# Attention and a two-expert router on one core: the two heads of a pair in one product of 128 rows, with block-diagonal keys and values

## The chip, the cores and the metric

The kernel runs on one core of one Trainium2 chip. A core has five engines that work side by side and signal one another with semaphores: TensorE (PE, matrix products, with weight loads shown as PEld), VectorE (DVE), ScalarE (ACT), GpSimd (POOL) and SyncE (SP), and 16 DMA engines that move data between the chip's memory, the on-chip memory SBUF and the product memory PSUM. The metric is the time of one execution in microseconds. Before the change it is 391.89 us, the median of 3 runs (388.24 to 396.87 us).

## The reference: what is computed

Two stages. The first is attention over 4 batches of 8 heads, 768 positions and 64 features. Positions are cut into 24 chunks of 32 queries. A chunk sees 8 memory keys of its batch and head and a window of 56 positions (16 to its left, its own 32, 8 to its right), cut off at the ends of the sequence:

```python
k_full = np.concatenate([mem_k, k_ctx], axis=2)
v_full = np.concatenate([mem_v, v_ctx], axis=2)
scores = scale * np.matmul(q_c, k_full.transpose(0, 1, 3, 2))
scores = scores - np.max(scores, axis=-1, keepdims=True)
a = np.exp(scores)
a = a / (np.sum(a, axis=-1, keepdims=True) + 1e-09)
out[:, :, c_start:c_end] = np.matmul(a, v_full)
```

The second stage takes the result as 3072 tokens of 512 features. Each token gets 8 noisy logits from two small matrices and given noise, and keeps the best two experts. The output is the sum of those two experts' results, `relu(x @ w1[e]) @ w2[e]` with 1024 hidden features, weighted by the softmax over the two logits.

## The kernel before

**Tiles.** A tile of attention is 256 positions of one batch (two groups of 128, index j) with all 8 heads, so there are 3 tiles a batch and 12 in all. Index i counts tiles, b = i // 3 is the batch and tp = i % 3 the tile in it. Heads go in 4 pairs; in SBUF the first head of a pair (par 0) has its 64 features on partitions 0 to 63, the second (par 1) on partitions 64 to 127.

**Loading.** Values, keys and queries of a batch are loaded in their natural layout by `load_batch` (lines 111 to 114). Keys and queries are turned by `turn` (lines 368 to 378), one unit for each pair, 4 units of keys and 4 of queries: 12 transposes of 128 positions by 64 features into PSUM, then a copy into `kT` or `qT`. Values take a way of their own: `spread_v` (line 347) copies them on POOL into `vp` with the heads in another order, `window_v` (line 353) stores them to a buffer `vd` in the chip's memory and loads them again, so that each chunk's window of 56 positions and its 8 memory values stand on partitions: the first heads of the pairs on partitions 0 to 63 of `vb`, the second heads on 64 to 127.

**A tile's work.** `scores` (line 380) has, for each j and pair, two products with the memory keys (one for each head) and eight with the keys: 4 chunks by 2 heads, each 64 rows (features) by 32 queries by 56 keys, placed at their own rows and columns of the array. A tile has 80 products. DVE then takes the maximum of each row and subtracts it, ACT takes the exponential (`exps`), PE turns the probabilities (`turn_p`), and `values` (line 426) multiplies them with `vb`: 64 products of 64 rows by 32 queries by 64 features, then a division by the sums (line 447) that writes `xrow`. `keep_x` (line 473) stores the rows of a tile to the chip's memory as `xd` for the experts, `turn_x` and `gate` compute the logits, and `Route` computes, batch by batch, which tokens go to which pair of experts.

**Order.** The order on PE, ACT, DVE and SP is the order of the program, written out by hand (line 504). The loop of lines 515 to 555 interleaves: in iteration i it computes the scores of tile i + 1, turns the probabilities of tile i, does the rest of tile i - 1, and the values of tile i. The query units of batch b + 1 are turned in iteration tp = 2, ahead of the scores of tile i + 1 (lines 525 to 528); its key units in tp = 1, behind the values (lines 543 to 546). POOL's DMA issues are kept in the order of the program too. There are two buffers each of `kT`, `qT`, `vb`, of the natural keys and queries `nat`, and of `xrow`, used in turn by even and odd batches. A framework that knows which instruction writes and reads which part of memory adds the waits, in the order of the program.

**Weights and scratch.** The weights of all 8 experts have one large tile, `w_all`: 65,536 columns of two bytes on 128 partitions, 8192 a expert, the first half of them for w1 and the second for w2. Attention's buffers `xrow`, `vb`, `vp`, `vn` and `nat` are cut from the upper end of the same tile (`scratch`, lines 94 to 103), from column 65536 downwards in the order in which they are named. Three experts are loaded while attention still runs, in iterations 6, 7 and 8 by the program's order:

```python
            if i in range(2 * TP, 2 * TP + 3):
                load_expert(i - 2 * TP)
            if tp == TP - 1 and b + 1 < B:
                for u in range(HP, 2 * HP):
                    o_, i_ = turn(b + 1, u)
```

The others are loaded from the end of the routing on. Then the experts' stage gathers tokens from `xd` (line 607), turns them (line 627) and runs two products for each expert (lines 646 and 655).

Of the kernel before, what the change touches and what calls it, by code (L numbers as in the profile page):

```python
# [22 lines left out]
def kernel(  # L23
# [14 lines left out]
    nc = tc.nc  # L38
    B, H, S, D = q.shape
# [30 lines left out]
    def pin(i):  # L70
        tc.keep_in_program_order(i)
# [32 lines left out]
    first_late = scol[0] // WE  # L104

    vd = [tc.dram_tile([S + CH, Dm], BF16, name=f"vd{i}") for i in range(2)]

# [22 lines left out]
    zeros = keep.tile([LC, Dm], BF16, name="zeros")  # L130
    nc.vector.memset(zeros, 0.0)
    for i in range(2):
        for r0, n in ((0, LC), (LC + S, CH - LC)):
# [7 lines left out]
    mvs = keep.tile([B * NM, H, D], F32, name="mvs")  # L141
# [55 lines left out]
    for i in range(2):  # L197
        nc.vector.memset(kT[i][:, :, 0:LC], 0.0)
        nc.vector.memset(kT[i][:, :, LC + S:SP], 0.0)

    mkT = keep.tile([128, HP, B * NM], BF16, name="mkT")
# [6 lines left out]
    nc.vector.tensor_copy(mkT, p_mk.rearrange("p c x b m -> p c (x b m)"))  # L208

    class Route:  # L210
        def __init__(self, g0, n, lg):
# [141 lines left out]
    def window_v(b):  # L353
        t, o = vb[b % 2], vd[b % 2]
        nc.sync.dma_start(out=o[LC:LC + S, :].rearrange("(p s) c -> p (s c)", s=SO), in_=vp)
        for par in range(2):
            p0 = par * 64
            cols = slice(par * 256, (par + 1) * 256)
            pin(nc.gpsimd.dma_start(out=t[p0:p0 + NM], in_=mvn[b * NM:(b + 1) * NM, cols].unsqueeze(1).to_broadcast([NM, NCH, 256])))
        for par in range(2):  # L360
            p0 = par * 64
            cols = slice(par * 256, (par + 1) * 256)
            for r0, n in ((0, CH), (CH, WIN - CH)):
                pin(nc.gpsimd.dma_start(out=t[p0 + NM + r0:p0 + NM + r0 + n],  # L364
                                        in_=o[r0:r0 + S, cols].rearrange("(c k) w -> k c w", k=CH)[0:n]))


    def turn(b, unit):
        x, pair = divmod(unit, HP)
        src = nat[b % 2][x]  # L370
        p_t = psT.tile([128, SO, 128], BF16, name="p_t", tag="ps_t")
        for s in range(SO):
            for par in range(2):
                nc.tensor.transpose(out=p_t[par * 64:par * 64 + 64, s, :],  # L374
                                    in_=src[:, 2 * pair + par, s * D:(s + 1) * D],
                                    identity=identb, tile_position=(0, par * 64))
        dst = qT[b % 2][:, pair, :] if x else kT[b % 2][:, pair, LC:LC + S]
        return dst.rearrange("c (p s) -> c p s", s=SO), p_t.rearrange("c s p -> c p s")

    def scores(t):  # L380
        b, tp = divmod(t, TP)
        q_, k_ = qT[b % 2], kT[b % 2]
        ps_s = psS.tile([128, 2, 2, HP, KW], F32, name="ps_s")
        for j in range(2):
            for pair in range(HP):
                tk = (2 * tp + j) * 128
                for par in range(2):
                    rows = slice(par * 64, par * 64 + 64)
                    nc.tensor.matmul(out=ps_s[:, par, j, pair, 0:NM], lhsT=q_[rows, pair, tk:tk + 128],  # L389
                                     rhs=mkT[rows, pair, b * NM:(b + 1) * NM], start=True, stop=True,  # L390
                                     tile_position=(par * 64, 0))
                for r in range(4):
                    for par in range(2):
                        rows = slice(par * 64, par * 64 + 64)
                        tr = tk + r * CH
                        nc.tensor.matmul(out=ps_s[r * CH:(r + 1) * CH, par, j, pair, NM:KW],  # L396
                                         lhsT=q_[rows, pair, tr:tr + CH],
                                         rhs=k_[rows, pair, tr:tr + WIN], start=True, stop=True,
                                         tile_position=(par * 64, r * CH))
        if tp == 0:  # L400
            nc.vector.memset(ps_s[0:CH, :, 0, :, NM:NM + LC], NEG)
        if tp == TP - 1:
            nc.vector.memset(ps_s[128 - CH:128, :, 1, :, KW - RC:KW], NEG)
        s3 = ps_s.rearrange("p a j c w -> p (a j c) w")
        mx = work.tile([128, 2 * H], F32, name="mx")
        nc.vector.tensor_reduce(out=mx, in_=s3, axis=AX, op=Alu.max)  # L406
        sc = work.tile([128, 2 * H, KW], F32, name="sc")
        nc.vector.tensor_tensor(out=sc, in0=s3, in1=bc(mx, KW), op=Alu.subtract)  # L408
        return sc

    def exps(sc):
        pb = work.tile([128, 2 * HP, 2, KW], BF16, name="pb")
        nc.scalar.activation(out=pb.rearrange("p x a w -> p a x w"), in_=sc.rearrange("p (a x) w -> p a x w", a=2),
                             func=Act.Exp, scale=scale)
        return pb

    def turn_p(pb):
# [8 lines left out]
    def values(t, pT, between=None):  # L426
        b, tp = divmod(t, TP)
        ps_g = psG.tile([128, 2, H], F32, name="ps_g", tag="ps_g")
        for x in range(2 * HP):
            j, pair = divmod(x, HP)  # L430
            nc.tensor.matmul(out=ps_g[:, j, 2 * pair:2 * pair + 2], lhsT=pT[:, x, :], rhs=ones2,
                             start=True, stop=True)
        ps_o = psO.tile([128, 2, 2, HP, D], F32, name="ps_o")
# [10 lines left out]
        nc.vector.reciprocal(rs, ps_g)  # L444
        xr = xrow[b % 2][:, 2 * tp:2 * tp + 2]
        for j in range(2):
            nc.vector.tensor_tensor(out=xr[:, j, 0:Dm].rearrange("p (c a d) -> p a c d", c=HP, a=2), in0=ps_o[:, :, j],  # L447
                                    in1=bc(rs[:, j].rearrange("p (c a) -> p a c", a=2), D), op=Alu.mult)
            if j == 0 and between is not None:
                between()  # L450
        return xr
# [52 lines left out]
    with tc.manual_schedule(engines={ET.PE, ET.Activation, ET.DVE, ET.SP}):  # L504
        spread_v(0)
        window_v(0)
        for u in range(2 * HP):
            o_, i_ = turn(0, u)
            (nc.scalar.copy if u % 2 else nc.vector.tensor_copy)(o_, i_)
        load_batch(1)  # L510
        spread_v(1)
        pbs[0] = exps(scores(0))
# [2 lines left out]
        for i in range(NT):  # L515
# [8 lines left out]
                load_expert(i - 2 * TP)  # L524
            if tp == TP - 1 and b + 1 < B:
                for u in range(HP, 2 * HP):
                    o_, i_ = turn(b + 1, u)
                    (nc.scalar.copy if u % 2 else nc.vector.tensor_copy)(o_, i_)
            if i + 1 < NT:
                sc = scores(i + 1)  # L530
# [11 lines left out]
            xrs[i] = values(i, pTs.pop(i), last)  # L542
            if tp == 1 and b + 1 < B:
                for u in range(HP):
                    o_, i_ = turn(b + 1, u)
# [352 lines left out]
```

## Time and profile before

| what | value |
|---|---|
| median of 3 runs | 391.89 us (388.24 to 396.87) |
| the profiled execution | 393.52 us |
| its span | 391.8 us, 8846 instructions |
| PE busy | 307.5 us (78%), 3868 products |
| DVE busy | 169.3 us (43%) |
| ACT busy | 120.2 us (31%) |
| POOL busy | 129.5 us (33%) |
| moved by DMA | 54.07 MB, mean 138 GB/s |
| score products with keys, line 396 | 768, busy 24.3 us |
| score products with memory keys, line 389 | 192, busy 17.9 us |
| value products, line 439 | 768, busy 10.0 us |
| key copies after the first batch, line 546 | 12, busy 8.7 us |

Engines overlap, so their busy times don't add up to the span, and a busy time is an average over stages. What counts is which wait ends last in each stage. A group is named by its line, engine and operation, with out<-in by the program's names. In a timeline or a chain, idle time is put down to its releaser, the event that ended it; "issue" is idle time in which the engine waited for nothing that the profile shows. A granted clock of 1.0 is TensorE's full speed.

### The profile page before, as it was taken

Reading aid. Unit: us, or ns where it says so; the run is one execution under the profiler, and the core shown is the slowest. Engines: PE = TensorE matmul, PEld = TensorE weight load, DVE = VectorE, ACT = ScalarE, POOL = GpSimd, SP = SyncE. Lnnn points to the kernel's source line nnn. Section 1 sums busy time; section 2 is a strip of 40 time slices with the busy share of each in tenths; the row PEclk is TensorE's granted clock in tenths of the full one; section 3 lists DMA queues with packets and bytes.
Section 4 is the critical chain, followed back from the end, with each engine's and each line's share of the span. In section 5 each row is a group of like instructions: output and inputs, shape, how many; then the busy total and the mean of one; then the engine's idle time right before and its main releaser. Section 6 shows DMA issues by size and latency. Waiting matters only on the chain.

```text
span 391.8 us, 8846 instructions
## 1 busy us (share of the span) xinstructions
PE 307.5 (78%) x3868; PEld 199.1 (51%) x3868; DVE 169.3 (43%) x393; ACT 120.2 (31%) x182; POOL 129.5 (33%) x168
## 2 busy tenths in 40 slices
PE   0267765866758455379999999999988999999991
PEld 0256654755646343246555446666445666555540
DVE  2345444867657369734123411595321134313230
ACT  1122633540452323013432143312224411244310
POOL 6353234325520003476236522063272023201122
PEclk9999965565585555559999999999999999999997
DMA  9999999999999992039999970712039941100012
GB/s 125 238 141 189 213 157 222 219 150 217 204 182 218 217 205 66 12 98 190 240 209 247 228 153 14 122 44 95 24 114 173 210 97 73 68 5 2 21 43 74
DMA packets 42957, 54.07 MB, mean 138 GB/s; under 512 B 7607, under 2 KB 33271, under 8 KB 42912
## 3 DMA queue, kind: packets, MB, share of 16 engines
q0 software_dynamic: 34240, 46.82, 66.1%
q10 hardware_dynamic: 7136, 3.02, 3.6%
q1 hardware_dynamic: 1536, 3.61, 2.5%
q8 instruction: 32, 0.52, 0.5%
q14 instruction: 13, 0.11, 0.1%
HBM read 70.39 MB, written 13.96 MB: 215 GB/s over the span
## 4 chain that ended last, share of the span: by engine, by line
PE 30%; issue 17%; DMA 5%; POOL 4%; DVE 3%; POOLq 1%
PE p_h L646 16%; PE p_y L655 12%; DMA out_dram<-y,main_dst 5%; POOL out_dram L613 2%; PE p_xt L627 1%; POOL xt L607 1%; DMA xt<-xd,main_src 1%; POOL w_all L771 0%; POOL w_all L770 0%; DVE w_all L447 0%; POOLq L893 0%; DVE oh_l L306 0%; DVE c L227 0%; DVE mm L224 0%; DVE c L229 0%
## 5 line engine op out<-in xcount | busy, mean ns | idle before, releaser
L655 PE MATMUL p_y<-w_all,h 128*128 128x512 bf16 x464 | 103.9, 379 | 2.4 <-ACT y L659 2.4
L646 PE MATMUL p_h<-xTt,w_all 128*128 128x384 bf16 (+2 forms) x640 | 102.3, 319 | 0.0
L646 PEld LDWEIGHTS <-w_all 128*128 128x128 bf16 x704 | 66.8, 99 | 38.0 <-issue 2.1
L634 ACT ACTIVATE h<-p_h 128x512 bf16<-128x512 f32 (+1 forms) x82 | 44.7, 545 | 102.9 <-PE p_h L646 90.7
L655 PEld LDWEIGHTS <-h 128*128 128x128 bf16 x464 | 44.9, 98 | 53.5 <-issue 2.7
L632 DVE TENSOR_SCALAR h<-p_h 128x512 bf16<-128x512 f32 (+1 forms) x50 | 31.3, 626 | 89.4 <-PE p_h L646 86.4
L613 POOL DMA_INDIRECT out_dram<-y,main_dst x28 | 31.1, 1110 | 104.1 <-DVE y L661 84.0
L661 DVE SCALAR_TENSOR_TENSOR y<-p_y,main_w,y 128x512 f32<-128x512 f32 x28 | 21.0, 750 | 37.4 <-PE p_y L655 32.3
L607 POOL DMA_INDIRECT xt<-xd,main_src x28 | 27.3, 975 | 25.4 <-PE p_xt L627 16.1
L396 PE MATMUL ps_s<-kT,qT 64*32 64x56 bf16 x768 | 24.3, 220 | 13.3 <-issue 13.3
L374 PE MATMUL p_t<-identb,w_all 128*64 128x128 bf16 x384 | 20.8, 295 | 15.4 <-DMA w_all<-in_k_dram 8.2
L659 ACT ACTIVATE y<-p_y,main_w 128x512 f32<-128x512 f32 x28 | 19.1, 687 | 41.0 <-PE p_y L655 35.1
L423 ACT COPY pT<-p_p 128x1024 bf16<-128x1024 bf16 x12 | 12.1, 1012 | 58.2 <-PE p_p L420 58.2
L374 PEld LDWEIGHTS <-w_all 128*64 128x64 bf16 x384 | 18.7, 160 | 16.5 <-DMA w_all<-in_k_dram 8.3
L349 POOL COPY w_all<-w_all 128x1536 bf16<-128x1536 bf16 x8 | 13.0, 1658 | 35.0 <-DMA w_all<-in_v_dram 35.0
L389 PE MATMUL ps_s<-mkT,qT 64*128 64x8 bf16 x192 | 17.9, 184 | 4.4 <-DVE sc L408 2.9
L364 POOL DMA_DIRECT2D w_all<-vd x16 | 11.9, 748 | 25.0 <-DMA vd<-w_all 25.0
L406 DVE TENSOR_REDUCE mx<-ps_s 128x16 f32<-128x1024 f32 x12 | 14.7, 1223 | 8.9 <-PE ps_s L396 8.6
L447 DVE TENSOR_TENSOR w_all<-ps_o,rs 128x512 bf16<-128x512 f32 x24 | 15.6, 686 | 6.6 <-PE ps_o L439 6.0
L439 PE MATMUL ps_o<-w_all,pT 64*32 64x64 bf16 x768 | 10.0, 233 | 9.8 <-issue 9.8
L396 PEld LDWEIGHTS <-qT 64*32 64x32 bf16 x768 | 11.8, 96 | 11.2 <-issue 9.6
L389 PEld LDWEIGHTS <-qT 64*128 64x128 bf16 x192 | 10.0, 100 | 14.2 <-issue 5.8
(163 smaller groups left out, 300.3 us busy)
## 6 DMA issues: line engine op xcount, KB each, us to landing
w_all<-in_moe_w_dram POOLq DMA_DIRECT2D x16, 1024.0 KB
w_all<-in_moe_w_dram POOLq DMA_DIRECT2D x8, 512.0 KB
w_all<-in_v_dram POOLq DMA_DIRECT2D x4, 768.0 KB
w_all<-in_k_dram POOLq DMA_DIRECT2D x4, 768.0 KB
w_all<-in_q_dram POOLq DMA_DIRECT2D x4, 768.0 KB
vd<-w_all SPq DMA_DIRECT2D x4, 768.0 KB, 7.4
w_all<-vd POOLq DMA_DIRECT2D x8, 384.0 KB
xd<-w_all ACTq DMA_DIRECT2D x11, 256.0 KB, 7.6
```

The source lines that it names most:

```text
L374: nc.tensor.transpose(out=p_t[par * 64:par * 64 + 64, s, :], in_=src[:, 2 * pair + par, s * D:(s + 1) * D], identity=identb, tile_position ...
L389: nc.tensor.matmul(out=ps_s[:, par, j, pair, 0:NM], lhsT=q_[rows, pair, tk:tk + 128], rhs=mkT[rows, pair, b * NM:(b + 1) * NM], start=True ...
L396: nc.tensor.matmul(out=ps_s[r * CH:(r + 1) * CH, par, j, pair, NM:KW], lhsT=q_[rows, pair, tr:tr + CH], rhs=k_[rows, pair, tr:tr + WIN], s ...
L447: nc.vector.tensor_tensor(out=xr[:, j, 0:Dm].rearrange("p (c a d) -> p a c d", c=HP, a=2), in0=ps_o[:, :, j], in1=bc(rs[:, j].rearrange("p ...
L607: i = nc.gpsimd.indirect_dma_start(out=xts[key].bitcast(I32), out_offset=None, in_=xd, in_offset=bass.IndirectOffsetOnAxis(ap=ix, axis=0))
L613: i = nc.gpsimd.indirect_dma_start(out=out, out_offset=bass.IndirectOffsetOnAxis(ap=ix, axis=0), in_=y, in_offset=None, bounds_check=N - 1 ...
L632: nc.vector.tensor_scalar(out=out_, in0=in_, scalar1=0.0, scalar2=None, op0=Alu.max)
L634: nc.scalar.activation(out=out_, in_=in_, func=Act.Relu)
L646: nc.tensor.matmul(out=o, lhsT=w(kp * F + f * 128, 128), rhs=x[:, kp], start=(kp == 0), stop=(kp == KP - 1))
L655: nc.tensor.matmul(out=p, lhsT=h[:, (f * n + j) * 128:(f * n + j + 1) * 128], rhs=w(KP * F + f * Dm, Dm), start=(f == 0), stop=(f == FB - 1))
L659: nc.scalar.activation(out=y, in_=p, func=Act.Copy, scale=weight)
L661: nc.vector.scalar_tensor_tensor(out=y, in0=p, scalar=weight, in1=y, op0=Alu.mult, op1=Alu.add)
```

## The change

Both heads of a pair go into one product whose 128 rows are the features (for values: the keys) of both heads. For this the keys `kT`, the memory keys `mkT` and the values `vb` get a further index for the head and are block-diagonal: the part of head 0 is zero on partitions 64 to 127, the part of head 1 on partitions 0 to 63. A product's output then has both heads side by side: 16 columns for memory keys, 112 for keys, 128 for values. The zeros are written once at the start. `kT` and `qT` become one buffer each, `vb` doubles, `vp` and the small staging tile `mvs` change places between the scratch and memory of their own, and a turned unit of keys is copied in two halves. The layouts of the scores and of the values' result follow.

```diff
     xrow = [scratch(SO * Dm).rearrange("p (s r) -> p s r", s=SO) for _ in range(2)]
-    vb = [scratch(NCH * HP * D).rearrange("p (c w) -> p c w", c=NCH) for _ in range(2)][::-1]
-    vp = scratch(H * SO * D)
     vn = scratch(H * SO * D).rearrange("p (h c) -> p h c", h=H)
+    vb = [scratch(2 * NCH * HP * D).rearrange("p (a c w) -> p a c w", a=2, c=NCH) for _ in range(2)][::-1]
     nat = [[scratch(H * SO * D).rearrange("p (h c) -> p h c", h=H) for _ in range(2)] for _ in range(2)]
...
+    vp = keep.tile([128, H * SO * D], BF16, name="vp")
...
-    kT = [keep.tile([128, HP, SP], BF16, name=f"kT{i}") for i in range(2)]
-    qT = [keep.tile([128, HP, S], BF16, name=f"qT{i}") for i in range(2)]
...
+    kT = keep.tile([128, HP, 2, SP], BF16, name="kT")
+    qT = keep.tile([128, HP, S], BF16, name="qT")
+    for par in range(2):
+        nc.vector.memset(kT[own(par), :, 1 - par, :], 0.0)
+        nc.vector.memset(kT[own(par), :, par, 0:LC], 0.0)
+        nc.vector.memset(kT[own(par), :, par, LC + S:SP], 0.0)
+        nc.vector.memset(vb[0][own(par), 1 - par], 0.0)
+        nc.scalar.copy(vb[1][own(par), 1 - par].rearrange("p (x c) w -> p x (c w)", x=NCH // 2),
+                       zeros[own(par), :].unsqueeze(1).to_broadcast([64, NCH // 2, Dm]))
...
-        dst = qT[b % 2][:, pair, :] if x else kT[b % 2][:, pair, LC:LC + S]
-        return dst.rearrange("c (p s) -> c p s", s=SO), p_t.rearrange("c s p -> c p s")
+        i = p_t.rearrange("c s p -> c p s")
+        if x:
+            return [(qT[:, pair, :].rearrange("c (p s) -> c p s", s=SO), i)]
+        return [(kT[own(par), pair, par, LC:LC + S].rearrange("c (p s) -> c p s", s=SO), i[own(par)]) for par in range(2)]
...
-                for par in range(2):
-                    rows = slice(par * 64, par * 64 + 64)
-                    nc.tensor.matmul(out=ps_s[:, par, j, pair, 0:NM], lhsT=q_[rows, pair, tk:tk + 128],
-                                     rhs=mkT[rows, pair, b * NM:(b + 1) * NM], start=True, stop=True,
-                                     tile_position=(par * 64, 0))
+                nc.tensor.matmul(out=ps_s[:, j, pair, :, 0:NM], lhsT=qT[:, pair, tk:tk + 128],
+                                 rhs=mkT[:, pair, :, b * NM:(b + 1) * NM], start=True, stop=True)
                 for r in range(4):
-                    for par in range(2):
-                        rows = slice(par * 64, par * 64 + 64)
-                        tr = tk + r * CH
-                        nc.tensor.matmul(out=ps_s[r * CH:(r + 1) * CH, par, j, pair, NM:KW],
-                                         lhsT=q_[rows, pair, tr:tr + CH],
-                                         rhs=k_[rows, pair, tr:tr + WIN], start=True, stop=True,
-                                         tile_position=(par * 64, r * CH))
+                    tr = tk + r * CH
+                    nc.tensor.matmul(out=ps_s[r * CH:(r + 1) * CH, j, pair, :, NM:KW], lhsT=qT[:, pair, tr:tr + CH],
+                                     rhs=kT[:, pair, :, tr:tr + WIN], start=True, stop=True, tile_position=(0, r * CH))
...
                 for r in range(4):
-                    for par in range(2):
-                        rows = slice(par * 64, par * 64 + 64)
-                        nc.tensor.matmul(out=ps_o[r * CH:(r + 1) * CH, par, j, pair, :],
-                                         lhsT=pT[rows, j * HP + pair, r * CH:(r + 1) * CH],
-                                         rhs=vb[b % 2][rows, (tp * 2 + j) * 4 + r, pair * D:(pair + 1) * D],
-                                         start=True, stop=True, tile_position=(par * 64, r * CH))
+                    nc.tensor.matmul(out=ps_o[r * CH:(r + 1) * CH, j, pair], lhsT=pT[:, j * HP + pair, r * CH:(r + 1) * CH],
+                                     rhs=vb[b % 2][:, :, (tp * 2 + j) * 4 + r, pair * D:(pair + 1) * D],
+                                     start=True, stop=True, tile_position=(0, r * CH))
...
             if tp == 1 and b + 1 < B:
                 for u in range(HP):
-                    o_, i_ = turn(b + 1, u)
-                    nc.scalar.copy(o_, i_)
+                    for o_, i_ in turn(b + 1, u):
+                        nc.scalar.copy(o_, i_)
```

More of the change, by code (lines that the diff above doesn't have):

```diff
@@ L129 @@
     make_identity(nc, identb)
-    zeros = keep.tile([LC, Dm], BF16, name="zeros")
+    vp = keep.tile([128, H * SO * D], BF16, name="vp")
+    zeros = keep.tile([128, Dm], BF16, name="zeros")
     nc.vector.memset(zeros, 0.0)
@@ L193, in bc, with own @@
         return ap.unsqueeze(len(ap.shape)).to_broadcast(list(ap.shape) + [n])
-    kT = [keep.tile([128, HP, SP], BF16, name=f"kT{i}") for i in range(2)]
-    qT = [keep.tile([128, HP, S], BF16, name=f"qT{i}") for i in range(2)]
[L197 to L201, printed above, removed]
+    def own(par):
+        return slice(par * 64, par * 64 + 64)
+    kT = keep.tile([128, HP, 2, SP], BF16, name="kT")
[7 more added lines that the diff above has]
+                       zeros[own(par), :].unsqueeze(1).to_broadcast([64, NCH // 2, Dm]))
+    mkT = keep.tile([128, HP, 2, B * NM], BF16, name="mkT")
+    nc.vector.memset(mkT, 0.0)
     p_mk = psT.tile([128, HP, 2, 2, NM], F32, name="p_mk", tag="ps_t")
@@ L207 @@
                              start=True, stop=True, tile_position=(0, par * 64))
-    nc.vector.tensor_copy(mkT, p_mk.rearrange("p c x b m -> p c (x b m)"))
+    for par in range(2):
+        nc.vector.tensor_copy(mkT[own(par), :, par, :], p_mk[own(par)].rearrange("p c x b m -> p c (x b m)"))
     class Route:
@@ L358, in window_v @@
             cols = slice(par * 256, (par + 1) * 256)
-            pin(nc.gpsimd.dma_start(out=t[p0:p0 + NM], in_=mvn[b * NM:(b + 1) * NM, cols].unsqueeze(1).to_broadcast([NM, NCH, 256])))
+            pin(nc.gpsimd.dma_start(out=t[p0:p0 + NM, par], in_=mvn[b * NM:(b + 1) * NM, cols].unsqueeze(1).to_broadcast([NM, NCH, 256])))
         for par in range(2):
@@ L363, in window_v @@
             for r0, n in ((0, CH), (CH, WIN - CH)):
-                pin(nc.gpsimd.dma_start(out=t[p0 + NM + r0:p0 + NM + r0 + n],
+                pin(nc.gpsimd.dma_start(out=t[p0 + NM + r0:p0 + NM + r0 + n, par],
                                         in_=o[r0:r0 + S, cols].rearrange("(c k) w -> k c w", k=CH)[0:n]))
@@ L373, in turn @@
             for par in range(2):
-                nc.tensor.transpose(out=p_t[par * 64:par * 64 + 64, s, :],
-                                    in_=src[:, 2 * pair + par, s * D:(s + 1) * D],
+                nc.tensor.transpose(out=p_t[own(par), s, :], in_=src[:, 2 * pair + par, s * D:(s + 1) * D],
                                     identity=identb, tile_position=(0, par * 64))
-        dst = qT[b % 2][:, pair, :] if x else kT[b % 2][:, pair, LC:LC + S]
-        return dst.rearrange("c (p s) -> c p s", s=SO), p_t.rearrange("c s p -> c p s")
+        i = p_t.rearrange("c s p -> c p s")
+        if x:
+            return [(qT[:, pair, :].rearrange("c (p s) -> c p s", s=SO), i)]
+        return [(kT[own(par), pair, par, LC:LC + S].rearrange("c (p s) -> c p s", s=SO), i[own(par)]) for par in range(2)]
     def scores(t):
         b, tp = divmod(t, TP)
-        q_, k_ = qT[b % 2], kT[b % 2]
-        ps_s = psS.tile([128, 2, 2, HP, KW], F32, name="ps_s")
+        ps_s = psS.tile([128, 2, HP, 2, KW], F32, name="ps_s")
         for j in range(2):
@@ L412, in exps @@
         pb = work.tile([128, 2 * HP, 2, KW], BF16, name="pb")
[L413 to L414 removed]
+        nc.scalar.activation(out=pb.rearrange("p x a w -> p (x a) w"), in_=sc, func=Act.Exp, scale=scale)
         return pb
@@ L432, in values @@
                              start=True, stop=True)
-        ps_o = psO.tile([128, 2, 2, HP, D], F32, name="ps_o")
+        ps_o = psO.tile([128, 2, HP, 2, D], F32, name="ps_o")
         for j in range(2):
@@ L507 @@
         for u in range(2 * HP):
-            o_, i_ = turn(0, u)
-            (nc.scalar.copy if u % 2 else nc.vector.tensor_copy)(o_, i_)
+            for n, (o_, i_) in enumerate(turn(0, u)):
+                (nc.scalar.copy if (u + n) % 2 else nc.vector.tensor_copy)(o_, i_)
         load_batch(1)
@@ L526 @@
                 for u in range(HP, 2 * HP):
-                    o_, i_ = turn(b + 1, u)
+                    o_, i_ = turn(b + 1, u)[0]
                     (nc.scalar.copy if u % 2 else nc.vector.tensor_copy)(o_, i_)
```

13 lines of the change are left out of this document (6 added, 7 removed).

## The prediction, made before the changed kernel had run

> **What bounds the kernel now.** I read the page's slices first, to divide the span into stages; then the chain that ended last, to see which wait ends each; then the timelines of PE and POOL around the last batch, and the stretches in which the DMA runs dry. The profiled execution took 393.52 us (span 391.8 us); the median of the three runs is 391.89 us, within their spread of 388.24 to 396.87. I work in the span's time and add the difference to the median.
>
> ```profile
> PE   0267765866758455379999999999988999999991
> PEclk9999965565585555559999999999999999999997
> DMA  9999999999999992039999970712039941100012
> ```
>
> A slice is 9.8 us. Attention fills slices 0 to 15: DMA full, PE broken up. From slice 18 the experts run PE without a gap. Between lies the routing. The change touches only the first stage, so its worth is how far it moves the first gather of the experts' tokens; in the chain that stands here:
>
> ```profile
> 151.69 0.17 DVE rs L444
> ...
> 164.23 1.09 POOL xt L607
> ...
> 170.94 0.61 PE p_xt L627 x4
> ```
>
> What sets PE's pace in attention is seen on its timeline at the first scores of batch 3 (the three columns ahead of the names are start, duration, engine; the bracket is idle time):
>
> ```profile
> 110.53 0.95 PE L374 MATMUL p_t<-identb,w_all 128*64 128x128 bf16 x24
> 112.60 0.86 PE L374 MATMUL p_t<-identb,w_all 128*64 128x128 bf16 x24 [1.12 <-ACT qT L528]
> 113.39 0.18 PE L389 MATMUL ps_s<-mkT,qT 64*128 64x8 bf16 x2
> 113.50 0.20 PE L396 MATMUL ps_s<-kT,qT 64*32 64x56 bf16 x2
> 116.91 0.21 PE L396 MATMUL ps_s<-kT,qT 64*32 64x56 bf16 x6 [3.21 <-issue]
> 117.06 0.19 PE L389 MATMUL ps_s<-mkT,qT 64*128 64x8 bf16 x2
> ...
> 117.36 0.19 PE L389 MATMUL ps_s<-mkT,qT 64*128 64x8 bf16 x2
> ```
>
> The 3.21 us of "issue" come inside a run of products that wait for nothing. There are twelve such gaps from 35 to 144 us (1.19, 0.89, 4.44, 1.59, 1.47, 3.83, 1.62, 3.21, 0.84, 1.40, 4.05, 1.20: 25.7 us). Counting matmuls between them gives 128 or a multiple each time (at matmul 352, 480, 864, 991, 1119, ... 2327, 2455, with a few records missing), that is 256 PE instructions, a product and its weight load being two. I read them as late instruction blocks while the DMA is full: 25.7 us over 17.4 blocks is 1.48 us a block. **A rule to weigh:** the Trainium skill (Runtime: NRT & Kernel Launch, Instruction fetch mechanics) says that instructions come in blocks of 256 and that the fetch is hidden. The block length agrees; "hidden" does not, with 1.48 us a block here. By the rule I would take no gap off below, and the sum would be 9.1 us higher.
>
> **The change, part by part.** *Fewer products.* Scores go from 80 products a tile (16 with memory keys, 64 with keys) to 40, values from 64 to 32: over 12 tiles 480 + 384 = 864 fewer, 6.75 blocks, 10.0 us by the row above. Each remaining product streams twice the columns. A group of ten score products takes 0.30 us (117.06 to 117.36), at clock 0.5 and, at 22.70 to 22.99 us, at clock 1.0, so columns do not bound it. A value tile's 64 products take 0.68 us (131.78 to 132.46). No row has a 128-row product on 32 columns. Low end, as cheap for each instruction as now: scores 1.2 us for 2.4, values 0.34. High end, four column tiles one after another at about 1.2 columns a ns (32 products of 512 columns take 6.91 us in the chain at clock 1.0; halved): 3.8 and 3.4 us. The nearest row, 48 transposes on 64-column tiles of 128 columns in 2.70 us at clock 0.5 (73.95 to 76.65), runs 56 ns each, half of 107: column tiles overlap. I take 2.0 for scores, 0.9 for values, so -0.4 and +0.2 us a tile. The Trainium skill (TensorEngine Tiling (Array Packing), Theoretical Speedup) speaks against the change: row tiling, given up here, is worth up to 2x for a contraction of 64. By it each group's 0.18 us of key products doubles, 4.3 us for the three tiles that count below.
>
> *Keys split in two.* A turned key unit is copied in two halves of 64 partitions and the same 768 elements. After the first batch all eight copies are ACT's, where four took 2.91 us (line 546, at 108.00): +2.9 us ahead of the exponentials in each of three batches, 8.7 us, if nothing covers them. In the first batch the eight are shared with DVE, eight of 0.80 to 0.96 us against four, about 4 us for 2.8; the queries land only at 19.99, so nothing is late.
>
> *Zeroing.* Two DVE memsets of 64x3072 and two of 64x1584 words, about 3 and 1.5 us each (128x168 takes 0.20 us at line 188), and two ACT copies of 6144 elements, 5 to 6 us each (768 take 0.80). ACT is idle until 15.05, DVE for some 6 us before 11.44. I cost it at 0 to 2 us at the start; the wait for the queries of batch 1 (1.49 us at 46.00) and the wait below absorb it.
>
> *Scratch memory.* This decides. Scratch is cut downwards from column 65536 of the weights' tile. Before, 36,864 columns go, down to 28672, above experts 0 to 2 (0 to 24575). Now the value windows double: 6144 + 3072 + 24576 + 12288 = 46,080, down to 19456, so the queries of odd batches (19456 to 22527) and part of their keys lie **inside expert 2** (16384 to 24575). The loop issues that expert at i = 8, line 524, before line 527 turns the queries of batch 3. In program order the write is first, so the first of the four query turns must wait for the half of expert 2 called w1 and the second for w2: the boundary, column 20480, falls inside head 2. Neither wait is there before. The other direction, the load waiting for the key turn at i = 7 (107 to 110 us), costs nothing: its issue stands at 112.12, with megabytes ahead of it.
>
> ```profile
> 109.51 0.76 POOL L74 DMA_DIRECT2D w_all<-in_moe_w_dram  x1 [0.62 <-DMA w_all<-vd]
> 112.12 0.90 POOL L75 DMA_DIRECT2D w_all<-in_moe_w_dram  x1 [1.85 <-DMA w_all<-vd]
> ```
>
> When does expert 2 land? Six transfers of 1024 KB stand on this queue from 105.54 on; in the stretches (last three columns: clock, DMA share, GB/s) the traffic ends here:
>
> ```profile
> 115.00:145.00 30.00, 18.00 (x522) 14.46 (x522) 16.46 (x35) 9.18 (x11) 0.00 (x0) 0.53 1.17 215
> 145.00:146.00 1.00, 0.00 (x0) 0.00 (x0) 0.90 (x6) 0.00 (x0) 0.00 (x0) 0.50 0.87 186
> 146.00:147.00 1.00, 0.87 (x16) 0.87 (x16) 0.91 (x3) 0.00 (x0) 0.00 (x0) 0.50 0.74 135
> 147.00:148.00 1.00, 1.00 (x14) 1.00 (x12) 0.93 (x5) 0.00 (x0) 0.00 (x0) 0.50 0.43 72
> ```
>
> So about 147.5. Three stores of 256 KB (line 476, at 120.29, 130.49, 140.49) share the stretch; now they sit behind the wait: 0.79 MB at 215 GB/s, 3.7 us earlier. With some start delay I take 144.5. PE stops at 110.53 at the latest, some 34 us before, so all that the other parts do up to there, gains of blocks and losses of copies, is hidden. Behind the waiting transpose on PE are scores of tile 9, then turned probabilities and values of tile 8; ACT's copy of those, DVE's maxima and routing of batch 1, and POOL's first gather follow.
>
> *The stretch behind the wait.* After 144.5: three query units of 12 transposes at 56 ns, 2.0 us; scores of tile 9 start at 146.5. Before, from their start (113.39) to the first gather (164.23) is 50.8 us, with gaps of 3.21, 0.84, 1.40, 4.05 and 1.20. The DMA is now nearly idle, and no "issue" gap stands on PE between 145 and 164, when it was idle. I take off 9.1: the 1.20 lies beside the twenty DVE operations of the routing (142.2 to 145.8) that line 444 follows, and 0.4 goes to PE's wait for DVE's one-hot (0.70 us before 126.89). Products: 3 x -0.4 + 4 x 0.2 = -0.4, which I leave within the rounding. That is 41.7 us: first gather at 188.2, 24.0 us late. Behind it the experts' stage is unchanged: 393.5 + 24 = 417.5 for a profiled execution, **416 us** by the median.
>
> **Rivals.** *The wait costs nothing* (other side). If expert 2 were in place when PE comes to the query turn, or the turn were ordered ahead of the load, the wait is nothing; it begins to cost at a landing of about 110. Then 391.9 - 10.0 (blocks) + 8.7 (copies) - 2.4 (products): 388, within 2%; with the copies hidden by late blocks about 379. For it: 26 us of gaps are PE's pace. Against it: 6.3 MB behind a window that is still landing at 112. Chance 0.11. Then the change also does what it says: under my forecast the queries of batch 3 are partly expert weights, so that batch's scores are another computation.
>
> *Column tiles do not overlap, and the wait stands.* 3 x 1.4 + 4 x 2.7 = 15 us on top: 431. The half-column transposes speak against it. Chance 0.10.
>
> *Forecast*, 0.79. Its bounds: landing at 141 and products at their low end (3 x 0.8 + 4 x 0.56 = 4.6 us less), 408; landing at 149 with half of the gaps staying, 425. The range 408 to 428 takes these in and leaves out most of the two rivals, 0.2 together. A measurement of this kernel tells about 2% from no change: faster 0.04, same 0.08, slower 0.88.
>
> **What the changed profile would show.** PE idle for some 30 us ahead of line 384's transposes, released by the weights' DMA, ending near 144; no "issue" gaps after it; ACT's key copies near 5.8 us a batch; PE rows of scores near 2 us a tile; the first gather near 188 and the experts' stage as long as now. I am wrong if that idle time is under 15 us, if the gaps return behind it, or if the experts' stage moves.

## The result and the profile after

The changed kernel takes 420.1 us (median of 4 runs, 418.11 to 423.03) against 392.79 us before (4 runs, 388.24 to 396.87): ratio 1.074, 95% interval 1.061 to 1.088. Throughout, medians are of all executions, while ratios and intervals compare only the faster ones of each kernel, those within 1.5% of its fastest. The profiled execution took 418.51 us, its span is 416.9 us, 25.1 us longer than before. First the page's slices, each now 10.4 us:

```profile
PE   0258789588100089643999999999999999999991
PEclk9999855858655555555799999999999999999997
DMA  9999899899899900101799998071214991110011
```

In slices 10 to 13 PE stands nearly still while the DMA is full; the attention of the last batch comes behind, with the DMA empty. The timeline of PE names the cause (start, duration, and in brackets the idle time before):

```profile
141.59 0.95 PE L384 MATMUL p_t<-identb,w_all 128*64 128x128 bf16 x13 [34.40 <-DMA w_all<-in_moe_w_dram]
146.64 1.49 PE L384 MATMUL p_t<-identb,w_all 128*64 128x128 bf16 x23 [4.09 <-DMA w_all<-in_moe_w_dram]
148.37 0.85 PE L384 MATMUL p_t<-identb,w_all 128*64 128x128 bf16 x12 [0.25 <-ACT qT L527]
149.16 0.20 PE L397 MATMUL ps_s<-mkT,qT 128*128 128x16 bf16 x1
149.28 0.28 PE L401 MATMUL ps_s<-kT,qT 128*32 128x112 bf16 x4
149.50 0.19 PE L397 MATMUL ps_s<-mkT,qT 128*128 128x16 bf16 x1
```

The first query unit waits 34.40 us for one half of expert 2 and then runs 13 transposes, the 12 of its unit and one of the next. The fourteenth reads the other half and waits 4.09 us more, as the column count had it. All columns of these queries (19456 to 22527) lie inside expert 2 and are read after it has landed, so the changed kernel computes the scores of batch 3 from expert weights in place of its queries. The first gather, which opens the experts' stage, moves from 164.23 to 191.58 us:

```profile
191.58 1.09 POOL L606 DMA_INDIRECT xt<-xd,main_src  x1 [2.55 <-DVE main_dst L487]
```

From there to the end it is 225.3 us, against 227.6 before. So the loss arises ahead of the gather, and the experts' stage gives nothing to it.

One thing was not foreseen. The groups of score and value products before (first fence) and after (second fence; out<-in xcount, busy and mean, idle time and its releaser) show that all "issue" gaps are gone, also those ahead of 107 us, where the DMA is as full as before (197 GB/s from 40 to 107 us in both kernels):

```profile
L396 PE MATMUL ps_s<-kT,qT 64*32 64x56 bf16 x768 | 24.3, 220 | 13.3 <-issue 13.3
L439 PE MATMUL ps_o<-w_all,pT 64*32 64x64 bf16 x768 | 10.0, 233 | 9.8 <-issue 9.8
```

```profile
L401 PE MATMUL ps_s<-kT,qT 128*32 128x112 bf16 x384 | 26.8, 270 | 0.0
L439 PE MATMUL ps_o<-w_all,pT 128*32 128x128 bf16 x384 | 11.9, 298 | 0.0
```

### The profile page after: what moved, and what is told of

Read it like the earlier page. It is cut to its first block, busy times and chain, and to the rows that moved or that the text cites. A ratio compares the mean times of both kernels' runs of the same rounds, so it can differ in the third digit from the quotient of the medians.

```text
span 416.9 us, 7144 instructions
## 1 busy us (share of the span) xinstructions
PE 312.2 (75%) x3004; PEld 197.5 (47%) x3004; DVE 178.9 (43%) x401; ACT 143.0 (34%) x198; POOL 128.0 (31%) x168
## 4 chain that ended last, share of the span: by engine, by line
PE 28%; issue 16%; DMA 5%; POOL 4%; DVE 2%; POOLq 1%
PE p_h L645 15%; PE p_y L654 12%; DMA out_dram<-y,main_dst 4%; POOL out_dram L612 2%; PE p_xt L626 1%; POOL xt L606 1%; DMA xt<-xd,main_src 1%; POOL w_all L770 0%; POOL w_all L769 0%; DVE w_all L446 0%; POOLq L892 0%; DVE oh_l L316 0%; DVE c L237 0%; DVE mm L234 0%; DVE c L239 0%
## 5 line engine op out<-in xcount | busy, mean ns | idle before, releaser
L384 PEld LDWEIGHTS <-w_all 128*64 128x64 bf16 x384 | 17.8, 148 | 64.6 <-DMA w_all<-in_moe_w_dram 38.8
L606 POOL DMA_INDIRECT xt<-xd,main_src x28 | 27.3, 976 | 25.1 <-PE p_xt L626 15.8
L401 PE MATMUL ps_s<-kT,qT 128*32 128x112 bf16 x384 | 26.8, 270 | 0.0
L527 DVE COPY qT<-p_t 128x768 bf16<-128x768 bf16 x6 | 5.7, 958 | 41.5 <-PE p_t L384 41.4
L359 POOL COPY vp<-w_all 128x1536 bf16<-128x1536 bf16 x8 | 11.5, 1467 | 36.6 <-DMA w_all<-in_v_dram 36.6
L321 POOL TENSOR_TENSOR vals<-ohp,facts 128x1008 bf16<-128x1008 bf16 (+2 forms) x3 | 2.8, 938 | 62.4 <-DVE facts L289 62.4
L397 PE MATMUL ps_s<-mkT,qT 128*128 128x16 bf16 x96 | 18.4, 192 | 3.6 <-DVE sc L411 2.9
L545 ACT COPY kT<-p_t 64x768 bf16<-64x768 bf16 x24 | 19.0, 793 | 1.9 <-PE p_t L384 1.5
L527 ACT COPY qT<-p_t 128x768 bf16<-128x768 bf16 x6 | 4.7, 800 | 39.0 <-PE p_t L384 38.9
```

What stands on the lines that cost most here:

```text
L384: nc.tensor.transpose(out=p_t[own(par), s, :], in_=src[:, 2 * pair + par, s * D:(s + 1) * D], identity=identb, tile_position=(0, par * 64))
L397: nc.tensor.matmul(out=ps_s[:, j, pair, :, 0:NM], lhsT=qT[:, pair, tk:tk + 128], rhs=mkT[:, pair, :, b * NM:(b + 1) * NM], start=True, sto ...
L401: nc.tensor.matmul(out=ps_s[r * CH:(r + 1) * CH, j, pair, :, NM:KW], lhsT=qT[:, pair, tr:tr + CH], rhs=kT[:, pair, :, tr:tr + WIN], start= ...
L606: i = nc.gpsimd.indirect_dma_start(out=xts[key].bitcast(I32), out_offset=None, in_=xd, in_offset=bass.IndirectOffsetOnAxis(ap=ix, axis=0))
```

## The experiments

Each is compared with the kernel before on the same chip. Three chips were used, and they differ by themselves (the kernel before: 390.37 us on the first, 393.40 on the second, 396.67 on the third), so ratios are used across chips.

**The load behind the turn.** The loop's two blocks change places:

```diff
-            if i in range(2 * TP, 2 * TP + 3):
-                load_expert(i - 2 * TP)
             if tp == TP - 1 and b + 1 < B:
                 for u in range(HP, 2 * HP):
                     o_, i_ = turn(b + 1, u)[0]
                     (nc.scalar.copy if u % 2 else nc.vector.tensor_copy)(o_, i_)
+            if i in range(2 * TP, 2 * TP + 3):
+                load_expert(i - 2 * TP)
```

> The changed kernel with the load of expert 2 issued behind the turn of the queries of batch 3 (two blocks of the loop change places; memory and products as changed). Theory (the loss is PE's wait for expert 2): the query turn starts near 107 us as in the changed kernel and runs through; the rest of attention takes 45 to 55 us, so the first gather comes at 153 (no issue gaps, as in the changed kernel) to 162 (gaps come back while the DMA is full): 381 to 390 us, ratio 0.97 to 1.00 to the kernel before. Rival (the wider products, the copies or the zeros cost the time, and the wait only shows it): still above 405 us.

Measured: 382.98 us against 390.37, ratio 0.979 (0.975 to 0.984). The first gather is at 155.49 us. No issue gap is left although the DMA is full in that stretch (219 GB/s from 115 to 145 us).

**Other memory, same order.** The natural buffers of even and odd batches are exchanged, so that expert 2 lies over batch 2's:

```diff
-    nat = [[scratch(H * SO * D).rearrange("p (h c) -> p h c", h=H) for _ in range(2)] for _ in range(2)]
+    nat = [[scratch(H * SO * D).rearrange("p (h c) -> p h c", h=H) for _ in range(2)] for _ in range(2)][::-1]
```

> The changed kernel with the natural keys and queries of even and odd batches exchanged in memory, so that expert 2 lies over those of batch 2, which have been turned long before its load; program order as changed. Theory: as the kernel with the turn first, 381 to 390 us, since only the overlap counts and not the order of the two statements. Rival (some other cost of the order or of the changed parts): above 405 us, or more than 2% apart from the kernel with the turn first.

Measured: 382.81 us, ratio 0.976 (0.970 to 0.982), first gather at 156.00 us. The two repairs, one of order and one of place, agree within their intervals: the loss is the overlap in combination with the order, and nothing else in the change costs more than it brings.

**The overlap alone, in the kernel before.**

```diff
+    scratch(9216)
     nat = [[scratch(H * SO * D).rearrange("p (h c) -> p h c", h=H) for _ in range(2)] for _ in range(2)]
```

> The kernel before with 9216 unused columns cut from the scratch ahead of the natural keys and queries, so that they lie where the change puts them, over expert 2. Nothing else is changed, and the queries of batch 3 are overwritten by weights as in the changed kernel. Theory: the query turn waits from about 110 to 146.6 us, then 2.5 us of turning and 42 to 44 us to the first gather, near 191: 418 to 421 us, ratio 1.065 to 1.075, the whole loss without any of the wider products. Rival (the loss needs the changed products, copies or zeros): 388 to 397 us.

Measured: 419.88 us against 390.37, ratio 1.074 (1.067 to 1.082), the ratio of the change itself to the third decimal. Its PE timeline has the same two waits on the old transposes:

```profile
143.52 0.95 PE L375 MATMUL p_t<-identb,w_all 128*64 128x128 bf16 x13 [32.69 <-DMA w_all<-in_moe_w_dram]
148.57 1.49 PE L375 MATMUL p_t<-identb,w_all 128*64 128x128 bf16 x23 [4.10 <-DMA w_all<-in_moe_w_dram]
```

First gather at 192.41 us. With the wait in place it hardly matters which products run: what the new products gain ahead of it is hidden, as the 34 us of slack had it. (This kernel, too, reads expert weights in place of the queries of batch 3, and so does the next one.)

**A shorter wait.** Expert 2 is loaded ahead of experts 0 and 1, which move to iterations 9 and 10:

```diff
-            if i in range(2 * TP, 2 * TP + 3):
-                load_expert(i - 2 * TP)
+            if i in range(2 * TP + 2, 2 * TP + 5):
+                load_expert((2, 0, 1)[i - 2 * TP - 2])
```

> The changed kernel with expert 2 loaded ahead of experts 0 and 1; it is still issued ahead of the query turn. Theory (the time follows the landing): expert 2 now has 4.2 MB less ahead of it, some 20 us at 209 GB/s, lands near 127 instead of 146.6, and the first gather moves by the same: near 172, 398 to 402 us; up to 9 us later if issue gaps come back while experts 0 and 1 are still on their way. Rival (PE is held by something else in that time): 417 to 421 us, no move.

Measured: 398.93 us, ratio 1.021 (1.015 to 1.026).

```profile
122.00 0.95 PE L384 MATMUL p_t<-identb,w_all 128*64 128x128 bf16 x13 [15.23 <-DMA w_all<-in_moe_w_dram]
127.05 1.49 PE L384 MATMUL p_t<-identb,w_all 128*64 128x128 bf16 x23 [4.10 <-DMA w_all<-in_moe_w_dram]
```

PE is released 19.6 us earlier than in the changed kernel (127.05 for 146.64), the first gather comes 20.1 us earlier (171.49 for 191.58), the span is 20.5 us shorter (396.4 for 416.9). The time follows the landing one to one.

**Where the gaps come from: an empty DMA.** The kernel before, with the loads of experts 0 to 2 behind attention:

```diff
-            if i in range(2 * TP, 2 * TP + 3):
-                load_expert(i - 2 * TP)
...
+    for e in range(3):
+        load_expert(e)
+
     actx.close()
```

> The kernel before with the loads of experts 0 to 2 issued behind attention instead of in iterations 6 to 8, so that from about 116 us the DMA is nearly idle; PE's instructions are the same. Theory (an issue gap is a block of 256 PE instructions that arrives late because the DMA is full): the gaps up to 107 us stay (1.2, 0.9, 4.4, 1.6, 1.5, 3.8, 1.6), the five behind it (3.21, 0.84, 1.40, 4.05, 1.20) go, and the first gather would come some 9 us earlier, near 155, if POOL did not issue the loads ahead of it. Rival (gaps come with these products themselves, whatever the DMA does): the five stay. The total time says little here, since the experts then wait for weights.

Measured (one run): 407.25 us; the total is that of experts that wait for weights. The gaps up to 107 us stay, 16.2 us in nine; the five behind are gone. The stretches (the last three columns are clock, DMA share, GB/s) show the DMA that goes with it, and the timeline the last gap:

```profile
112.00:125.00 13.00, 9.15 (x293) 7.25 (x288) 10.60 (x21) 4.71 (x6) 0.00 (x0) 0.74 0.35 56
125.00:140.00 15.00, 10.91 (x297) 9.63 (x294) 11.38 (x36) 6.81 (x9) 0.00 (x0) 0.50 0.11 38
```

```profile
107.16 0.30 PE L439 MATMUL ps_o<-w_all,pT 64*32 64x64 bf16 x13 [0.64 <-issue]
113.01 1.20 PE L374 MATMUL p_t<-identb,w_all 128*64 128x128 bf16 x24 [0.89 <-ACT qT L526]
```

So the same products have no gap when the DMA is far from full (35 and 11% busy): the gap needs a full DMA. PE is not slower there: counted in stretches of 128 products, it takes 4.4 to 5.7 us each from 114.25 to 133.74 us. The kernel before with the overlap shows the same behind its wait: from 151 to 170 us, at 40 GB/s, stretches of 3.8 to 5.7 us and no gap.

**Where the gaps come from: PE's pace.** The exchanged buffers, with the value products taken back to 64 rows:

```diff
-                    nc.tensor.matmul(out=ps_o[r * CH:(r + 1) * CH, j, pair], lhsT=pT[:, j * HP + pair, r * CH:(r + 1) * CH],
-                                     rhs=vb[b % 2][:, :, (tp * 2 + j) * 4 + r, pair * D:(pair + 1) * D],
-                                     start=True, stop=True, tile_position=(0, r * CH))
+                    for par in range(2):
+                        nc.tensor.matmul(out=ps_o[r * CH:(r + 1) * CH, par, j, pair, :],
+                                         lhsT=pT[own(par), j * HP + pair, r * CH:(r + 1) * CH],
+                                         rhs=vb[b % 2][own(par), par, (tp * 2 + j) * 4 + r, pair * D:(pair + 1) * D],
+                                         start=True, stop=True, tile_position=(par * 64, r * CH))
```

> The changed kernel with the natural buffers exchanged, and the value products taken back to 64 of 64 rows a tile (reading the nonzero blocks of the same doubled buffer); scores keep 40 products a tile. PE has 384 products more. Theory A (a block of 256 PE instructions takes some 6 us to arrive while the DMA is full, and a gap stands only where PE gets through the block before in less): a tile has 136 products besides turns, so a block lasts about as long as a tile, 7 us and more, and the gaps stay nearly all away, under 5 us in all: 382 to 386 us. Theory B (a gap of 1.48 us a block, as the prediction had it): some 14 blocks in attention, about 20 us of gaps, and 390 us or more. Theory C (the 64-row products bring the gaps): gaps within or behind the values, 10 us or more.

Measured: ratio 0.978 (0.968 to 0.988), median 387.07 us against 393.40. Four gaps, 4.8 us in all:

```profile
62.19 0.30 PE L440 MATMUL ps_o<-w_all,pT 64*32 64x64 bf16 x14 [1.44 <-issue]
...
91.87 0.31 PE L440 MATMUL ps_o<-w_all,pT 64*32 64x64 bf16 x15 [0.93 <-issue]
...
108.24 0.53 PE L440 MATMUL ps_o<-w_all,pT 64*32 64x64 bf16 x38 [0.76 <-issue]
...
118.74 1.39 PE L384 MATMUL p_t<-identb,w_all 128*64 128x128 bf16 x22 [1.67 <-issue]
```

Its profiled execution (span 387.7 us) is at the long end of its runs (381.88 to 389.9), so the exact total is not to be leaned on; but it is 4.8 us and not the 20 us of a fixed price a block, as theory A had it and against B. It is also under the 10 us of theory C, although three of the four gaps do stand within the values. A time of its own for the value products does not come out: the ratio is that of the kernel with both wider.

**Shared key copies.** The exchanged buffers, with the halves of a key unit on ACT and DVE in turn:

```diff
-                    for o_, i_ in turn(b + 1, u):
-                        nc.scalar.copy(o_, i_)
+                    for n, (o_, i_) in enumerate(turn(b + 1, u)):
+                        (nc.scalar.copy if (u + n) % 2 else nc.vector.tensor_copy)(o_, i_)
```

> The changed kernel with the natural buffers exchanged (no overlap with expert 2) and the eight half copies of each batch's keys shared by ACT and DVE instead of all on ACT. Theory (the key copies stand on the path three times): the copies end about 3 us earlier in each of three batches, so 375 to 379 us against 382.8 for the same kernel with all copies on ACT. Rival (they lie beside PE's and DVE's other work, or DVE's own work is pushed back as much): 381 to 384.

Measured: 393.43 us, ratio 1.005 (1.001 to 1.009): some 3% slower than with all copies on ACT, a plain miss. The timelines of ACT (first fence) and DVE show why:

```profile
78.82 1.61 ACT L545 COPY kT<-p_t 64x768 bf16<-64x768 bf16 x2 [5.93 <-DVE kT L545]
82.44 1.61 ACT L545 COPY kT<-p_t 64x768 bf16<-64x768 bf16 x2 [2.01 <-DVE kT L545]
```

```profile
77.84 0.94 DVE L545 COPY kT<-p_t 64x768 bf16<-64x768 bf16 x1
80.46 1.94 DVE L545 COPY kT<-p_t 64x768 bf16<-64x768 bf16 x2 [1.68 <-ACT kT L545]
84.08 0.96 DVE L545 COPY kT<-p_t 64x768 bf16<-64x768 bf16 x1 [1.68 <-ACT kT L545]
```

The second half of a unit waits for the first: the two engines take turns instead of working together. And the first DVE copy stands behind DVE's routing and the division of the values, until 77.84, while the key units were being turned from 73.31 on.

**Zeros later**, on top of that:

```diff
-        nc.vector.memset(vb[0][own(par), 1 - par], 0.0)
...
+            if u in (HP - 1, 2 * HP - 1):
+                nc.vector.memset(vb[0][own(u // HP), 1 - u // HP], 0.0)
```

> As the kernel with shared copies, and the two DVE memsets of the first value window moved from the front of DVE's queue behind the key copies and behind the query copies of batch 0. Theory (the changed start is 4 us late, first probabilities turned at 36 us and not at 32, because the key copies stand behind these memsets, and nothing absorbs it): the first exponentials 3 to 4 us earlier and the time 3 us under that of the shared copies alone. Rival (a wait for the first batches' data absorbs it): the same time within 1 us.

Measured: ratio 1.005 (1.002 to 1.009), no gain; first exponentials at 33.41 us, not earlier than the 31.94 without it. Moving the zeros alone mends nothing while the halves take turns (first key copies end at 22.1, and a memset then stands ahead of the query copies).

**The start mended**: zeros later, and in the first batch both halves of a unit on one engine; later batches as changed.

```diff
-            for n, (o_, i_) in enumerate(turn(0, u)):
-                (nc.scalar.copy if (u + n) % 2 else nc.vector.tensor_copy)(o_, i_)
+            for o_, i_ in turn(0, u):
+                (nc.scalar.copy if u % 2 else nc.vector.tensor_copy)(o_, i_)
```

> The changed kernel with the natural buffers exchanged, and in the first batch both halves of a key unit copied by one engine (units on DVE and ACT in turn), with the two DVE memsets of the first value window behind the key and the query copies; later batches' key copies all on ACT as changed. Theory (the start is 4 us late because the second half of a unit waits for the first on the other engine, and the copies stand behind DVE's memsets; nothing absorbs it): first exponentials near 28 to 29 us instead of 32.1, and 378 to 380 us against 382.8. Rival (the load of the first keys and queries, or of batch 1, absorbs the start): 382 to 384.

Measured: 384.57 us against 396.67 on this chip, ratio 0.967 (0.962 to 0.972), the lowest ratio of the study, against 1.074 for the change as it stands. The first exponentials come at 29.61 us for 32.12. Most of that is given back. PE reaches batch 2 earlier and then waits for its loads,

```profile
69.93 2.13 PE L383 MATMUL p_t<-identb,w_all 128*64 128x128 bf16 x36 [0.82 <-DMA w_all<-in_k_dram]
...
78.18 1.49 PE L383 MATMUL p_t<-identb,w_all 128*64 128x128 bf16 x24 [3.31 <-DMA w_all<-in_q_dram]
```

the next turned probabilities come at 84.23 us for 85.83, and the first gather at 155.22 us for 156.00; where the rest went between these two I have not traced. So both expectations hold in part, and whether it beats the exchanged buffers alone is not settled: the intervals touch (0.970 to 0.982 and 0.962 to 0.972).

**Whole units shared** in the later batches as well:

```diff
-                    for o_, i_ in turn(b + 1, u):
-                        nc.scalar.copy(o_, i_)
+                    for o_, i_ in turn(b + 1, u):
+                        (nc.vector.tensor_copy if u % 2 else nc.scalar.copy)(o_, i_)
```

> As the kernel with the mended start, and in the later batches the key units on ACT and DVE in turn, both halves of a unit on one engine. Theory (the shared copies lost 10 us because of the wait between the halves on two engines, and eight copies in a row on ACT, 6.5 us, still stand on the path three times): 4 to 8 us under the mended start, 371 to 376. Rival (what costs is that copies on DVE push its own work back): as slow as the shared copies, 388 us or more.

Measured: 385.7 us, ratio 0.971 (0.967 to 0.975), the same as the mended start within the intervals. Neither expectation: without the wait between halves the loss of the shared copies is gone, which leaves that wait as the larger part of it; but no gain comes either. In batch 1 the exponentials behind the copies are earlier (74.57 us for 77.31), and the next turned probabilities are not (85.21 for 84.23): PE waits 3.30 us for the queries of batch 2, until 78.69, so the load and not the copies was on the path there. (This profiled execution, 389.69 us, is at the long end of its runs, 384.43 to 391.38.)

## Why the prediction was right

The forecast was 416 us with 408 to 428; 420.1 was measured, for the reason given. By its steps:

| step | predicted | measured |
|---|---|---|
| PE waits for expert 2 ahead of the query turn, first and second unit | yes, from 110.5 at the latest | 34.40 and 4.09 us, from 107.2 |
| expert 2 landed | 144.5 | 146.64 |
| three query units turned | 2.0 us | 2.5 us (to 149.16) |
| scores of tile 9 to the first gather | 41.7 us | 42.4 us |
| first gather | 188.2 | 191.58 |
| experts' stage | unchanged | 2.3 us shorter |
| loss | 24.0 us | 25.1 us in the span, 27.3 us between medians |

**The wait** is shown twice over: by the overlap alone in the kernel before (1.074) and by the shorter wait (20 us for 20 us). **The landing** was 2.1 us late with the last window's loads issued 2.2 us later than before (104.76 for 102.59). That lag begins with the values of batch 1, which landed 1.3 us later (36.85 for 35.58) although they were asked for 0.4 us earlier; I have not tried why. **The stretch behind** came out within a microsecond, which is partly luck. No gap returned, as said. The products were mis-sized: a score tile takes 2.72 us (149.16 to 151.88), not 2.0, and 2.4 before; a value tile 0.98 us (162.93 to 163.91), not 0.9, and 0.68 before. Three of the one and four of the other add 2.2 us where I had 0.4 less; but the gaps of this stretch went whole, 10.7 us, where I had taken off 9.1. And the loss in the span comes near the forecast because the experts' stage gave back 2.3 us that I had not foreseen: the first gather itself is 27.35 us late and not 24.0.

On the Trainium skill's up to 2x for row tiling (TensorEngine Tiling (Array Packing), Theoretical Speedup): at clock 0.5 the key products of a group take 0.22 us (149.28 to 149.50) for 0.19 before (117.17 to 117.36). The trace agrees as far as "up to": what is given up here is 1.16 times and not 2, since the column tiles still overlap.

**Terms that were wrong without harm**, because the wait hid them or because they only price the rival:

- *Blocks.* I took the gaps as a fixed price, 1.48 us a block, so that 6.75 fewer blocks would save 10.0 us. The blocks did go: the fetching queue moved 0.41 MB in 25 packets for 0.52 MB in 32. But all 25.7 us went with them. What a gap is can be read from that queue's packets in the trace before: each of the twelve gaps ends 1.3 to 1.7 us after a packet of 16 KB has landed (the one that ends at 116.91: on its way from 113.94 to 115.44), so PE stands until its next 256 instructions have come. How long they take is not one number. Counted in stretches of 128 products (a few records are missing), six of the blocks between two gaps took 5.92 to 6.20 us, but the four with the largest gaps, ending at 61.32, 89.84, 116.91 and 137.78, took 8.1 to 10.0 us, and two (from 48.24 and from 95.76) took 4.96 and 4.75 us and have none of the twelve gaps at their end, the DMA full in all of them. The packet sets off 1.5 to 7.1 us after PE began the block before (49.77 for 48.24, 113.94 for 106.88); what decides that is not shown. So the time of a fetch is to be compared with PE's own time for the block before, and not added: PE stalls only where it is the faster. A tile now has 40 + 32 products for 80 + 64, so PE takes longer over a block. Both sides were tried: an empty DMA takes the gaps away with the old products, and 32 products a tile put back bring 4.8 us. The Trainium skill's sentence that the fetch is hidden (Runtime: NRT & Kernel Launch, Instruction fetch mechanics) holds in the changed kernel and not in the kernel before.
- *Key copies.* Eight take 6.47 us for 2.91, +3.6 us a batch and not +2.9. That they stand on the path holds in one kernel and not in the other: with the exchanged buffers alone PE waits for them in batch 1 (1.12 us until 78.81, 1.09 until 80.43), while with the mended start it waits there for the load of the queries, and sharing whole units gained nothing.
- *The start.* 0 to 2 us and absorbed, I said; it is 4.1 us (first exponentials at 32.22 us for 28.07) and is not absorbed in batch 1: its key units are turned from 44.5 us on, before from 41.4. PE waits 4.30 us in the first key turn because the PSUM buffer of the turned memory keys is freed by a DVE copy behind the 2.62 us memset, and the copies of halves take turns (what stands in PSUM leaves it here by copies of DVE and ACT; none of the profile's DMA transfers goes to or from it):

```profile
19.50 1.49 PE L384 MATMUL p_t<-identb,w_all 128*64 128x128 bf16 x24 [4.30 <-DVE mkT L218]
21.64 0.85 PE L384 MATMUL p_t<-identb,w_all 128*64 128x128 bf16 x12 [0.65 <-DVE kT L508]
23.45 0.85 PE L384 MATMUL p_t<-identb,w_all 128*64 128x128 bf16 x12 [0.96 <-ACT kT L508]
```

- *The rival without the wait* was put at 388 us, within 2%, and 379 with the copies hidden; the two repairs measured 383 us, 2.1 and 2.4% faster than before. The sign was open there, and it is a gain: of the 25.7 us of gaps that are gone, 8 us arrive at the first gather (156.00 for 164.23). The late start is part of the rest; the whole of it I have not taken apart.

What stays open: how much of those 8 us is due to the scores and how much to the values (the one run with 64-row values has too wide an interval), and why the experts' stage is 2.3 us shorter in the changed kernel; single executions of the changed kernel differ by more (418.11 to 423.03 us).

## What to carry to other kernels

Where buffers share memory with something that is loaded early, recompute the addresses after every change of a size, and look for a write that now stands ahead of a read in program order: the framework turns it into a wait, and what the reader then finds is the new data. Two lines moved, or one changed, repair it here, and the change then gains about 2% where it lost 7%. Price a fetch of instructions as a time to be compared with PE's own time for 256 instructions (here some 5 to 10 us with the DMA full), not as so much for each block; and before halves of one buffer are shared by two engines, see in the trace that they don't wait for each other.

## What the runs showed of the hardware that was not expected

- With the DMA full (about 160 to 220 GB/s) PE waited for its next 256 instructions at the end of six blocks of 5.92 to 6.20 us and of four of 8.1 to 10.0 us (106.88 to 116.91 the longest); with the DMA at 38 to 56 GB/s blocks of 4.4 to 5.7 us have no gap.
- Four 128-row products on 32-column tiles with 112 columns take 0.22 us at clock 0.5 and 0.16 us at clock 1.0 (97.96 to 98.12 us), so halving the clock costs 1.4 times and not 2.
- A copy of 768 elements takes as long on 64 partitions (793 ns mean on ACT) as on 128 (812 ns): splitting a copy by partitions doubles its cost.
